# Squared-ReLU attention and top-1 experts on one core: end-of-chunk steps, start and order of the mixed steps rearranged

## The chip, the core and the metric

The kernel runs on one core of a Trainium2 chip. The metric is device time in microseconds (us); lower is better. The core has the engines TensorE (PE in the rows, with PEld for its weight loads), VectorE (DVE), ScalarE (ACT), GpSimd (POOL) and SyncE (SP, which issues most DMAs). Each takes its instructions in the order of its own queue.

## What is computed

With B = 8, S = 2496, D = 256, 64 query columns, E = 8 experts, capacity 80 and F = 1024:

```
scores = (1/S) * z @ z.T          # z [B, S, 64]
attn   = max(scores, 0) ** 2
x      = u * (attn @ v)           # u, v [B, S, 256]
idx    = argmax(x @ w_gate), gate = its softmax weight
per expert: the 80 tokens of the largest gate,
    out[tok] = gate * (max(x[tok] @ w1[e], 0) @ w2[e])
```

## The kernel before

**Tiling.** A *chunk* is 512 query columns of one batch (`b`, `qc` from 0 to 4; the fifth, `qc` = 4, has 448), 40 chunks in all. Its keys are 20 tiles of 128 rows, taken as 10 *pairs*. For a pair PE makes the scores (`scores`, matmuls L399, or L461 where only a half is needed), ACT the relu (L402) and the square (L405), ACT or DVE the rounded high part `ah` (L408, or L413 and L475 on DVE), and DVE the remainder `al` = a - ah (helper line L55). v is split likewise into two parts in `vt` (ACT L108, DVE L159). The scores are symmetric, so a block that another chunk needs too is transposed on DVE (L304, L316), written to DRAM, read back later (`blk`, `shared`) and only cast there (ACT L376, L471).

**Attention.** `attend_half` (L544) multiplies a pair in two *groups* of 12 matmuls: group 0 takes the passes with `ah` and then those with `al`, group 1 the `al` passes first. A matmul reads half the rows of a tile, so that two run side by side on the upper and lower half of the array; group 1 swaps which PSUM bank each half adds to, and waits for group 0 through an empty POOL instruction (L550). The two `acc` banks of a chunk are summed and multiplied by u at its end: `chunk_x_first` (DVE L569) reads one bank, `chunk_x_copy` (ACT L584) the other. The next chunk but one takes these banks over.

**Order of the work.** PE, ACT, DVE and SP follow an order that is written out by hand. After five opening steps with one chunk alone (`HALF` = 5) two *lanes* run side by side, the even chunks in the first and the odd ones in the second, shifted by half a chunk. A step `t` takes one pair of each lane (entries `e` and `e + 1`) and prepares two others (`e + 3`, `e + 4`): `begin` issues scores and relu, `middle` the square and the ACT cast of `ah`, `low` the DVE part (`al`), `turn` the transposes. Chunks end every fifth step; where an even one ends, `low(e + 3)` stands ahead of `chunk_x_first`, and where an odd one ends, the cast in `middle(e + 4)` stands ahead of `chunk_x_copy`. `z_and_v` splits z (`prep_zs`: L121 and L55 twice, 64 partitions each) and then v. `finish` spreads the rest of a chunk's end (`xb`, the second part of x, and the gate's logits, L684, reduced in L698) over the next chunk's steps. In 56 steps (14 of the half chunks, 4 steps each) one lane is 448 wide and the other 512; they are called mixed here.

**Start and end.** At the start 9 matmuls on zeros (`warm`, L186) precede the first scores, and `first` handles two pairs like any other. The last chunks run alone (`attend`, L515). The expert stage follows: GpSimd fetches each expert's rows by an indirect DMA (`token`, L1589) that DVE copies (L110, in `whole`), while the gate's last part (L744 to L771) and weight loads (L861) run.

Of the kernel before, what the change touches and what calls it, by code (L numbers as in the profile page):

```python
# [8 lines left out]
F32 = mybir.dt.float32  # L9
# [17 lines left out]
def attn_moe_kernel(ctx, tc, zT, uT, v, wg, w1, w2, out, seq, cap):  # L27
# [73 lines left out]
    def load_z(b, j):  # L101
        raw = zpool.tile([P, CH], F32, tag="zraw", name=f"zraw_{nid()}", bufs=1)
        nc.sync.dma_start(out=raw, in_=zT[b, :, j * CH:(j + 1) * CH])
        return raw

# [75 lines left out]
    nc.gpsimd.memset(idle, 0.0)  # L181

    def warm(n, pool, tag):
        wm = pool.tile([P, CH], F32, tag=tag, name=f"warm_{nid()}")
        for i in range(n):
            nc.tensor.matmul(wm, idle[:, :P], idle, start=True, stop=True)  # L186

    warm(9, ps_m, "m")
    raw12 = upool.tile([P, 2, CH], F32, tag="ut", name="raw12")
    nc.sync.dma_start(out=raw12[:, 0], in_=zT[0, :, CH:2 * CH])  # L190
    vraw0 = load_v(0, 0)
    nc.sync.dma_start(out=raw12[:, 1], in_=zT[0, :, 2 * CH:3 * CH])
    vraw1 = load_v(0, 1)
    raw34 = xpool.tile([P, 2, CH], F32, tag="xf", name="raw34")
    nc.sync.dma_start(out=raw34, in_=zT[0, :, 3 * CH:].rearrange("p (j t) -> p j t", j=2))
# [6 lines left out]
    wg_r = const.tile([P, DC, E], F32, name="wg_r")  # L202
# [22 lines left out]
    def constants_v():  # L225
        V.tensor_copy(out=wgs[:, :, 0], in_=wg_sb)
# [158 lines left out]
    def scores(b, qc, k):  # L385
# [18 lines left out]
        def square():  # L404
            nc.scalar.activation(out=a[:, :, :nc_], in_=a[:, :, :nc_], func=AF.Square)  # L405
            st["ah"] = pair_tile("ah", b, qc, k, bufs=4)
            if not on_v:
                nc.scalar.copy(out=st["ah"][:, :, :nq], in_=a[:, :, :nq])  # L408
# [18 lines left out]
        return square, low, turn  # L427
# [5 lines left out]
    def scores_rest(b, qc, k):  # L433
# [32 lines left out]
        def square():  # L466
            nc.scalar.activation(out=a, in_=a, func=AF.Square)
            st["ah"] = pair_tile("ah", b, qc, k, bufs=4)
# [17 lines left out]
        return square, low, None  # L486
# [32 lines left out]
    def attend_half(b, qc, p, group):  # L519
# [13 lines left out]
        for i, (k, x, a) in enumerate(mm):  # L533
            if start_up and i == len(ks):
                warm(2, ps_m, "m")
# [100 lines left out]
    def chunk_rows_last(b, qc):  # L636
# [16 lines left out]
        for ts_ in (slice(0, 2), slice(2, n)):  # L653
            nc.sync.dma_start(out=rows[r0 + ts_.start * P:r0 + ts_.stop * P].rearrange("(t p) w -> p t w", p=P),
                              in_=xq[:, ts_].rearrange("p t h d -> p t (h d)"))
        nc.sync.dma_start(out=rows[r0 + n * P + P - TAIL:r0 + QT * P],
                          in_=xq[P - TAIL:, n].rearrange("p h d -> p (h d)"))
# [31 lines left out]
    def chunk_sum(b, qc):  # L689
# [3 lines left out]
        for h, pl in enumerate(parts):  # L693
            o = lg_t[b][:, qc * QT:(qc + 1) * QT]
            if h:
                o = gp.tile([P, NT, E // 2], F32, tag="s4", name=f"lg2_{b}_{qc}")
                o = o.rearrange("p t e -> p (t e)")[:, :QT * E].rearrange("p (t e) -> p t e", e=E)
# [151 lines left out]
    def load_raw(e, which, part, after=None):  # L849
# [7 lines left out]
        if after:  # L857

            after.memset(raw[:, :1], 0.0)
        rv, src = raw_part(raw, e, which, part)  # L860
        nc.sync.dma_start(out=rv, in_=src)  # L861
# [16 lines left out]
    def loads(n, after=None):  # L878
        n = min(n, NR - len(ready) - len(halves))
        for p in pieces[:n]:  # L880
            ready.append((p, load_raw(*p, after)))
        del pieces[:n]
# [183 lines left out]
    if True:  # L1066
        prep_zm(0, 0, raw0)
# [25 lines left out]
        def middle(i):  # L1093
            b, qc, r = entries[i]
            if computed(i):
                pending[i][0]()
            else:
                pending[i] = None, mirrored(b, qc, 2 * pairs_of[b, qc][r]), None

        def low(i):  # L1100
            pending[i][1]()

        def turn(i):
            if pending[i][2]:
                pending[i][2]()
            del pending[i]

        def whole(i):
            begin(i)
            middle(i)  # L1110
            low(i)
# [13 lines left out]
        def z_and_v(t):  # L1125
# [3 lines left out]
            zb = b if tm < 2 else b + 1  # L1129
            if 0 < zb < B:  # L1130
# [5 lines left out]
            vb = b if tm < NP else b + 1  # L1136
            if 0 < vb < B:
                if tm in V_SPLIT:
                    g = V_SPLIT[tm]
                    prep_v(vb, g, v_raw.pop((vb, g)), nc.scalar, V)  # L1140
                if tm in V_LOAD:
                    v_raw[vb, V_LOAD[tm]] = load_v(vb, V_LOAD[tm])
# [22 lines left out]
        def group(i, g):  # L1165
            b, qc, r = entries[i]
            attend_half(b, qc, pairs_of[b, qc][r], g)
# [5 lines left out]
        for t in range(HALF):  # L1173
            if t == 0:
                begin(2)
            group(t, 0)
# [3 lines left out]
            first_parts(t)  # L1180
            group(t, 1)
# [6 lines left out]

        for t in range(HALF, END):
            e = HALF + 2 * (t - HALF)  # L1190
            n_end = t // HALF - 1 if t % HALF == HALF - 1 else None
            begin(e + 3)
            middle(e + 3)
            group(e, 0)
# [19 lines left out]
            low(e + 4)  # L1214
# [6 lines left out]
        for i in range(e, len(entries)):  # L1221
# [8 lines left out]
            if i == e + HALF + 1:  # L1230
                logits(n)
            if i + 2 < len(entries) and i > e:
# [5 lines left out]
            if i < e + HALF:  # L1238
                for j in range(2):
                    finished(*at(n), 2 * (i - e) + j)  # L1240
                    if i > e or j:
                        finished(*at(n - 1), NP + 2 * (i - e) + j)
# [200 lines left out]
    def steps_of(own, tl, tw, ps_t, ps_h):  # L1443
# [37 lines left out]
        def places_():  # L1481


            for n in ("cnt", "exc", "rin", "base"):
                small[n] = tl.tile([P, E], F32, name=f"{n}_all")
            for e in range(E):
# [31 lines left out]
        def many_rows():  # L1518
            le = le_g[1][:, :, 1:]
            tt(le, le, tot[:, es], ALU.mult)  # L1520
            V.tensor_reduce(out=small["exc"][:, es], in_=le, axis=AX.X, op=ALU.add)
# [55 lines left out]

        def token(i):
# [9 lines left out]
            xg = tw.tile([P, 2, D], U16, tag="xg", name=f"xg_{i}{own}", bufs=6)  # L1588
            nc.gpsimd.indirect_dma_start(  # L1589
# [3 lines left out]
            xg_t[i] = [xg, tok, j]  # L1593

        def target(i):
# [4 lines left out]
            xg, tok, j = xg_t[i]  # L1600
# [120 lines left out]
        def flags_end():  # L1721
            flags2(ps_t, "t")

        early_steps = (ps_t, ps_h, (ffn1_high, ffn1_low), places_, one_block, one_within, (many_blocks, many_counts, many_rows, many_within,
                       many_pe, many_fetch), pe_block, pe_fetch, warm_up, flags_v, flags_end, x_t, sl)
# [27 lines left out]
    def ahead(early_steps, steps):  # L1753
# [3 lines left out]
         flags_v, flags_end, x_t, sl) = early_steps  # L1757
        many_blocks, many_counts, many_rows, many_within, many_pe, many_fetch = many
# [21 lines left out]
        PL = nc.gpsimd  # L1780
        FIRST_J, LAST_J = range(FC // 2), range(FC // 2, FC)
        with tc.manual_schedule(engines={ET.Pool}):
# [17 lines left out]
            many_pe()  # L1800
            gate_near(B - 1, NQ - 1)
            gate_sum(B - 1, NQ - 1, NQ)
            whole(0)
            gate_store(P, NCOL - P, ps_t, "t")
            ffn_x(0)
            many_counts()
            many_fetch((2,))
            ffn_xl(0)
            ffn1(0, 0)
            whole(1)  # L1810
            many_rows()
            many_within()
            token(2)
            ffn_x(1)
            ffn_xl(1)
            ffn1(0, 1)
            token(3)
            loads(4, PL)
            ffn_h(0, 0)
            many_fetch((4, 6))  # L1820
            ffn1(1, 0)
            empty()
            target(0)
            target(1)
            token(4)
# [4 lines left out]
            ffn_x(2)  # L1830
            ffn_xl(2)
# [6 lines left out]
            spread(3)  # L1838
            for i in range(2, NU):
# [9 lines left out]
                if i == 2:  # L1849
                    token(6)  # L1850
                    token(7)
# [6 lines left out]
                if i + 1 < NU:  # L1858
                    cast(2)
                    lows(2)  # L1860
                ffn2(i - 1, FIRST_J)
# [58 lines left out]
```

## Time and profile before

| what | value |
|---|---|
| median of 3 runs | 1353.8 us (1351.98 to 1354.32) |
| profiled execution | 1355.23 us |
| its span, first to last instruction | 1353.3 us |
| mean granted TensorE clock | 0.993 of full |
| PE busy | 1329.6 us (98%) |
| DVE busy | 1085.8 us (80%) |
| ACT busy | 1020.1 us (75%) |

The profile is read by stage: the share of PE over the whole span says only that PE has work nearly all the time. The views used below are the page's busy times, the list of waits (which engine line stood idle for which other, in total, times, longest), windows (busy time of each engine in one stretch) and the timeline, whose rows give the start, the duration, and in brackets the idle time before with what ended it.

### The profile page before, as it was taken

The numbers are of one execution on the slowest core, as the hardware profiler recorded it, in microseconds if no ns is written. First come the engines' busy times: TensorE is split into PE (matmuls) and PEld (weight loads), VectorE is DVE, ScalarE is ACT, GpSimd is POOL, SyncE is SP. The second block draws the span as 40 slices with busy tenths as digits, with TensorE's granted clock in tenths as the row PEclk, the third lists the DMA queues.
The fourth block names the chain that finished last, engine by engine and source line by source line (L and its number), as shares of the span: only waits on it lengthen the run. The fifth ranks groups of instructions, "written<-read, shape, count | busy, mean of one in ns | idle before, by whom it ended". The sixth has DMA issues, their size and how long they took to land.

```text
span 1353.3 us, 32346 instructions
## 1 busy us (share of the span) xinstructions
PE 1329.6 (98%) x12887; PEld 1210.7 (89%) x12887; DVE 1085.8 (80%) x1667; ACT 1020.1 (75%) x1361; POOL 40.1 (3%) x42
## 2 busy tenths in 40 slices
PE   8999999999999999999999999999999999999997
PEld 5789998999899997999889998999889998898776
DVE  6777888887887888878878888878888778777886
ACT  6776787677867787776877778776877678777666
POOL 0000000000000000000000000000000000000065
PEclk8999999999999999999999999999999999999999
DMA  5799989999899998999899998999979997989945
GB/s 164 223 269 258 283 224 289 241 277 244 259 239 250 290 262 227 270 247 261 222 262 269 257 285 225 260 264 261 249 237 243 286 267 214 290 226 274 272 136 188
DMA packets 286013, 337.12 MB, mean 249 GB/s; under 512 B 96824, under 2 KB 206368, under 8 KB 275616
## 3 DMA queue, kind: packets, MB, share of 16 engines
q1 hardware_dynamic: 284832, 333.68, 93.8%
q8 instruction: 103, 1.69, 0.5%
q0 software_dynamic: 1024, 1.31, 0.3%
q14 instruction: 54, 0.44, 0.1%
HBM read 162.67 MB, written 135.48 MB: 220 GB/s over the span
## 4 chain that ended last, share of the span: by engine, by line
PE 83%; DVE 6%; ACT 4%; DMA 4%; issue 2%; SPq 0%; POOL 0%; DVEq 0%; POOLq 0%; ACTq 0%
PE acc L544 69%; PE s L399 9%; PE pl L684 2%; ACT a L402 1%; ACT a L405 1%; DVE al L55 1%; DMA blk<-y 1%; PE s L461 1%; DMA wraw<-w 1%; DVE x L304 1%; DVE vt L159 1%; PE warm L186 0%; ACT xf L584 0%; DMA y<-x 0%; PE op L1699 0%
## 5 line engine op out<-in xcount | busy, mean ns | idle before, releaser
L544 PE MATMUL acc<-ah,vt 64*128 64x512 f32 (+1 forms) x6004 | 845.9, 387 | 6.3 <-DVE xf L569 3.7
L544 PEld LDWEIGHTS acc<-ah,vt 64*128 64x128 f32 x6004 | 660.0, 185 | 60.1 <-DVE xf L569 6.7
L544 PE MATMUL acc<-al,vt 64*128 64x512 f32 (+1 forms) x3002 | 503.9, 389 | 0.4 <-DVE al L55 0.2
L55 DVE TENSOR_TENSOR al<-a,ah 128x1024 fp32r<-128x1024 f32 (+2 forms) x240 | 272.3, 1135 | 174.4 <-ACT ah L408 76.7
L544 PEld LDWEIGHTS acc<-al,vt 64*128 64x128 f32 x3002 | 340.0, 185 | 23.5 <-DVE al L55 1.1
L402 ACT ACTIVATE a<-s 128x512 f32<-128x512 f32 (+1 forms) x408 | 221.0, 594 | 141.7 <-PE s L399 138.8
L376 ACT CAST ah<-blk 128x1024 fp32r<-128x1024 f32 x160 | 167.1, 1047 | 102.7 <-PE acc L544 94.2
L55 DVE TENSOR_TENSOR al<-blk,ah 128x1024 fp32r<-128x1024 f32 x160 | 193.4, 1214 | 38.2 <-PE acc L544 10.7
L405 ACT ACTIVATE a<-a 128x1024 f32<-128x1024 f32 x204 | 216.3, 1060 | 6.3
L304 DVE STREAM_TRANSPOSE x<-a 128x512 f32<-128x512 f32 x320 | 207.6, 687 | 0.0
L408 ACT CAST ah<-a 128x1024 fp32r<-128x1024 f32 x160 | 168.0, 1050 | 5.8 <-PE acc L544 0.8
L399 PE MATMUL s<-zm,zs 64*128 64x512 f32 x960 | 148.7, 392 | 4.1 <-ACT a L402 4.1
L399 PEld LDWEIGHTS s<-zm,zs 64*128 64x128 f32 x960 | 107.2, 185 | 14.3 <-ACT a L402 5.7
L1589 POOL DMA_INDIRECT xg<-xs,tok x8 | 13.0, 1630 | 1294.7 <-ACT w2h L888 1286.1
L159 DVE TENSOR_TENSOR vt<-vraw,vt 128x1024 fp32r<-128x1024 f32 (+1 forms) x40 | 46.3, 1156 | 1.6 <-ACT vt L108 1.3
L55 DVE TENSOR_TENSOR xf<-xf,xb 128x1024 f32<-128x1024 f32 (+1 forms) x38 | 45.2, 1189 | 0.4
L55 DVE TENSOR_TENSOR xb<-xf,xb 128x1024 bf16<-128x1024 f32 (+1 forms) x38 | 45.1, 1186 | 0.2
L108 ACT CAST vt<-vraw 128x1024 fp32r<-128x1024 f32 (+3 forms) x56 | 44.9, 830 | 0.0
L594 ACT CAST xb<-xf 128x1024 bf16<-128x1024 f32 (+1 forms) x39 | 39.8, 1020 | 5.0 <-DVE xf L55 2.8
L602 ACT CAST xb<-xf 128x1024 bf16<-128x1024 f32 (+1 forms) x38 | 38.8, 1020 | 5.4 <-DVE xf L55 5.4
L399 PE MATMUL s<-zm 64*128 64x512 f32 x264 | 42.3, 400 | 0.4 <-ACT a L402 0.4
L413 DVE CAST ah<-a 128x1024 fp32r<-128x1024 f32 (+1 forms) x44 | 29.7, 675 | 14.1 <-ACT a L405 14.1
(190 smaller groups left out, 905.9 us busy)
## 6 DMA issues: line engine op xcount, KB each, us to landing
y<-x SPq DMA_DIRECT2D x80, 1024.0 KB, 6.9
blk<-y SPq DMA_DIRECT2D x320, 256.0 KB, 6.9
out<-idle SPq DMA_DIRECT2D x40, 512.0 KB, 7.8
vraw<-v SPq DMA_DIRECT2D x32, 512.0 KB, 9.3
zm<-zs SPq DMA_DIRECT2D x128, 128.0 KB, 4.8
ut<-uT SPq DMA_DIRECT2D x32, 512.0 KB, 6.8
xs<-xq SPq DMA_DIRECT2D x32, 512.0 KB, 6.6
wraw<-w SPq DMA_DIRECT2D x28, 512.0 KB, 5.3
```

What stands on the lines that cost most here:

```text
L55: V.tensor_tensor(out=o, in0=a, in1=b, op=op)
L108: eng.copy(out=o, in_=i)
L159: e1.tensor_tensor(out=vt[:, :nf, 1], in0=raw[:, :nf], in1=vt[:, :nf, 0], op=ALU.subtract)
L304: V.transpose(out=x[:, :, :, t].rearrange("p n k s -> p k n s"), in_=a)
L376: nc.scalar.copy(out=natural(ah), in_=src)
L399: nc.tensor.matmul(s, zk, zm[rows, :, y].rearrange("p h k t -> p k h t"), start=i == 0, stop=i == 2)
L402: nc.scalar.activation(out=a[:, h, :nc_], in_=s[:, :nc_], func=AF.Relu)
L405: nc.scalar.activation(out=a[:, :, :nc_], in_=a[:, :, :nc_], func=AF.Square)
L408: nc.scalar.copy(out=st["ah"][:, :, :nq], in_=a[:, :, :nq])
L544: ins = nc.tensor.matmul(acc[c], vt, mv, start=p == pairs[0] and group == 0 and i == 0, stop=p == pairs[-1] and group == 1 and i == len(mm ...
L594: nc.scalar.copy(out=xb[:, 0], in_=xf)
L602: nc.scalar.copy(out=xb[:, 1], in_=xr)
```

## The change

- The first pair's work is written anew (`first_pair`): relu, square and cast are divided between ACT and DVE, v is split in two halves, the warm-up has 8 matmuls and needs a smaller memset, scores stand inside the first group where two warm-up matmuls stood.
- z is loaded in two DMAs of 64 partitions that fetch only the halves which are used, and `prep_zs` splits 128 partitions at once: 2 DVE instructions where there were 4.
- `middle` is cut in two, the square and the cast. At the end of an odd chunk the cast follows `chunk_x_copy`; at the end of an even chunk `low(e + 3)` follows `chunk_x_first`; `z_and_v` splits v ahead of z.
- In a mixed step the second lane's second group, with its `low`, `turn`, `first_parts` and `z_and_v`, moves into the next step, behind `begin(e + 3)`, and the next step's first group is issued ahead of that.
- In the closing part `chunk_store`, `chunk_hi` and `chunk_lo` of the chunk that ended are taken earlier. In the expert stage the first rows are fetched ahead of the gate's last part, a small indirect DMA runs on GpSimd before, the four weight loads wait for the fourth fetch (`xg_t[3]`) and `token(6)`, `token(7)` come later.

```diff
     def prep_zs(b, j, raw):
-        for h in range(2):
-            rows = slice(h * HP, (h + 1) * HP)
-            src = tiles_of(raw)[rows, :, h]
-            V.tensor_copy(out=zs[rows, 0], in_=src)
-            tt(zs[rows, 1], src, zs[rows, 0], ALU.subtract)
+        src = raw.rearrange("p (k t) -> p k t", t=P)
+        V.tensor_copy(out=zs[:, 0], in_=src)
+        tt(zs[:, 1], src, zs[:, 0], ALU.subtract)
...
+    def first_pair(v_high, v_low):
...
+        nc.scalar.activation(out=a[:, 0], in_=ss[0], func=AF.Relu)
+        ts(a[:, 1], ss[1], 0.0, ALU.max)
+        v_high(0)
+        nc.scalar.activation(out=a[:, 0], in_=a[:, 0], func=AF.Square)
+        tt(a[:, 1], a[:, 1], a[:, 1], ALU.mult)
+        nc.scalar.copy(out=ah[:, 0], in_=a[:, 0])
+        V.tensor_copy(out=ah[:, 1], in_=a[:, 1])
+        v_low(0)
+        al = pair_tile("al", 0, 0, 0)
+        tt(al, a, ah, ALU.subtract)
...
-        first = scores(0, 0, 0)
-        first[0]()
-        first[1]()
-        prep_v(0, 0, vraw0, nc.scalar, V)
-        first = scores(0, 0, 2)
-        first[0]()
-        first[1]()
+        first_pair(v_high, v_low)
+        second_pair = scores(0, 0, 2)
+        v_high(1)
+        second_pair[0]()
+        v_low(1)
+        second_pair[1]()
+        second_pair[2]()
...
+        def second_lane(t):
+            e = HALF + 2 * (t - HALF)
+            group(e + 1, 1)
+            low(e + 4)
+            turn(e + 4)
+            first_parts(t)
+            z_and_v(t)
+
+        def mixed(t):
+            return t // HALF % NQ in (0, NQ - 1) and t % HALF < HALF - 1
+
         for t in range(HALF, END):
...
+            if t == HALF:
+                group(e, 0)
             begin(e + 3)
+            if mixed(t - 1):
+                second_lane(t - 1)
             middle(e + 3)
-            group(e, 0)
+            cast(e + 3)
+            if t > HALF and not mixed(t - 1):
+                group(e, 0)
...
             group(e, 1)
-            low(e + 3)
             if n_end is not None and n_end % 2 == 0:
                 chunk_x_first(*at(n_end))
                 chunk_x_copy(*at(n_end))
+            low(e + 3)
             turn(e + 3)
             middle(e + 4)
+            second = n_end is not None and n_end % 2 == 1
+            if not second:
+                cast(e + 4)
             finish(t, 1)
             transfers(e + 1)
+            if mixed(t):
+                group(e + 2, 0)
+                continue
             group(e + 1, 1)
-            if n_end is not None and n_end % 2 == 1:
+            if second:
                 chunk_x_first(*at(n_end))
                 chunk_x_copy(*at(n_end))
+                cast(e + 4)
             low(e + 4)
...
-            gate_near(B - 1, NQ - 1)
-            gate_sum(B - 1, NQ - 1, NQ)
             whole(0)
...
-            loads(4, PL)
             ffn_h(0, 0)
+            gate_store(P, NCOL - P, ps_t, "t")
+            loads(4, xg_t[3][3])
```

On DVE where chunk (0, 4), an even one, ends (names end in batch, chunk, pair; the trailing number is a counter). Before:

```order
184 L55 TENSOR_TENSOR xb_0_3_2274<-xf_0_3_2273,xb_0_3_2274 128x1024
185 L475 CAST ah_1_0_2_2699<-a_1_0_2_2687 128x512
186 L55 TENSOR_TENSOR al_1_0_2_2759<-a_1_0_2_2687,ah_1_0_2_2699 128x512
187 L55 TENSOR_TENSOR al_1_0_2_2759<-shared_137,ah_1_0_2_2699 128x512
188 L569 SCALAR_TENSOR_TENSOR xf_0_4_2762<-acc_0_4_0_1846,ut_0_4_2457 128x448
189 L413 CAST ah_1_1_4_2767<-a_1_1_4_2735 128x1024
```

and with the change:

```order
171 L55 TENSOR_TENSOR xb_0_3_2267<-xf_0_3_2266,xb_0_3_2267 128x1024
172 L610 SCALAR_TENSOR_TENSOR xf_0_4_2751<-acc_0_4_0_1840,ut_0_4_2452 128x448
173 L516 CAST ah_1_0_2_2705<-a_1_0_2_2673 128x512
174 L55 TENSOR_TENSOR al_1_0_2_2756<-a_1_0_2_2673,ah_1_0_2_2705 128x512
175 L55 TENSOR_TENSOR al_1_0_2_2756<-shared_140,ah_1_0_2_2705 128x512
176 L429 CAST ah_1_1_4_2760<-a_1_1_4_2728 128x1024
```

The read of the bank (L569, now L610) stood behind three instructions of `low` and now stands ahead of them.

On ACT where chunk (1, 0), an odd one, ends. Before:

```order
224 L405 ACTIVATE a_1_1_12_3246<-a_1_1_12_3246 128x1024
225 L408 CAST ah_1_1_12_3272<-a_1_1_12_3246 128x1024
226 L584 ACTIVATE xf_1_0_3280<-acc_1_0_1_2309 128x512
227 L376 CAST ah_1_2_2_3291<-blk_1_2_0_2974 128x1024
228 L402 ACTIVATE a_1_1_14_3323<-s_1_1_14_3324 128x512
```

and with the change:

```order
225 L419 ACTIVATE a_1_1_12_3238<-a_1_1_12_3238 128x1024
226 L625 ACTIVATE xf_1_0_3270<-acc_1_0_1_2304 128x512
227 L424 CAST ah_1_1_12_3274<-a_1_1_12_3238 128x1024
228 L390 CAST ah_1_2_2_3284<-blk_1_2_0_2968 128x1024
229 L416 ACTIVATE a_1_1_14_3316<-s_1_1_14_3317 128x512
```

The copy of the other bank (L584, now L625) and the cast have changed places.

On PE in a mixed step, where the second group of the 448 wide chunk's pair 0 ends. Before:

```order
1232 L544 MATMUL acc_0_4_1_1847<-ah_0_4_0_1728,vt_0_0_170 128x448
1233 L544 MATMUL acc_0_4_0_1846<-ah_0_4_0_1728,vt_0_0_170 128x448
1234 L544 MATMUL acc_0_3_0_1386<-al_0_3_16_1807,vt_0_4_673 128x512
1235 L544 MATMUL acc_0_3_1_1387<-al_0_3_16_1807,vt_0_4_673 128x512
1236 L544 MATMUL acc_0_3_0_1386<-al_0_3_16_1807,vt_0_4_673 128x512
```

and with the change:

```order
1226 L585 MATMUL acc_0_4_1_1841<-ah_0_4_0_1722,vt_0_0_149 128x448
1227 L585 MATMUL acc_0_4_0_1840<-ah_0_4_0_1722,vt_0_0_149 128x448
1228 L585 MATMUL acc_0_4_1_1841<-ah_0_4_2_1810,vt_0_0_149 128x448
1229 L585 MATMUL acc_0_4_0_1840<-ah_0_4_2_1810,vt_0_0_149 128x448
1230 L585 MATMUL acc_0_4_1_1841<-ah_0_4_2_1810,vt_0_0_149 128x448
```

The other lane's second group (`acc_0_3`) followed here; now the same lane's next pair comes first, and `acc_0_3` follows behind that and the next scores.

## Rows read from the trace of the kernel before

**Rows 1.** The list of waits (us in total, times, longest us).

```profile
PEld acc L544 <- DVE xf L569: 6.7, 10, 1.9
PEld acc L544 <- ACT xf L584: 5.5, 10, 0.6
PEld acc L544 <- DVE vt L159: 3.0, 4, 0.9
```

**Rows 2.** Timeline of the end of chunk (0, 4), an even one.

```profile
193.06 0.42 DVE L475 CAST ah<-a 128x512 fp32r<-128x512 f32 x1
...
193.88 1.07 PE L399 MATMUL s<-zm,zs 64*128 64x512 f32 x6
...
194.79 0.62 DVE L569 SCALAR_TENSOR_TENSOR xf<-acc,ut 128x448 f32<-128x448 f32 x1
...
195.47 0.77 PEld L544 LDWEIGHTS acc<-ah,vt 64*128 64x128 f32 x8 [0.96 <-DVE xf L569]
```

**Rows 3.** Timeline of the end of chunk (1, 0), an odd one.

```profile
227.62 1.05 ACT L408 CAST ah<-a 128x1024 fp32r<-128x1024 f32 x1
...
228.71 1.69 PE L544 MATMUL acc<-ah,vt 64*128 64x512 f32 x8
...
230.02 0.85 PE L544 MATMUL acc<-al,vt 64*128 64x512 f32 x4
```

**Rows 4.** Timeline of a split of v behind one of z.

```profile
337.19 0.24 DVE L121 CAST zs<-zraw 64x256 fp32r<-64x256 f32 x1
...
338.68 1.22 DVE L159 TENSOR_TENSOR vt<-vraw,vt 128x1024 fp32r<-128x1024 f32 x1
...
339.96 0.53 PEld L544 LDWEIGHTS acc<-ah,vt 64*128 64x128 f32 x6 [0.70 <-DVE vt L159]
```

**Rows 5.** Timeline of the start.

```profile
1.39 4.02 PE L186 MATMUL warm<-idle 128*128 128x512 bf16 x9 [1.39 <-POOL idle L181]
...
4.17 0.69 DVE L55 TENSOR_TENSOR zm<-zraw,zm 128x512 fp32r<-128x512 f32 x1
...
5.34 1.91 PE L399 MATMUL s<-zm 64*128 64x512 f32 x7
...
20.46 1.08 ACT L402 ACTIVATE a<-s 128x512 f32<-128x512 f32 x2 [4.17 <-PE s L399]
```

**Rows 6.** Groups by line and shape (count, then busy us and mean ns).

```profile
L405 ACT ACTIVATE a<-a 128x1024 f32<-128x1024 f32 x202 | 214.4, 1062 | 6.2
...
L569 DVE SCALAR_TENSOR_TENSOR xf<-acc,ut 128x512 f32<-128x512 f32 x33 | 22.6, 687 | 3.0 <-PE acc L544 2.8
...
L467 ACT ACTIVATE a<-a 128x512 f32<-128x512 f32 x29 | 18.4, 633 | 0.9
...
L475 DVE CAST ah<-a 128x512 fp32r<-128x512 f32 x29 | 12.1, 416 | 0.0
```

**Rows 7.** Windows: busy us of PE, PEld, DVE, ACT, POOL, clock, DMA share, GB/s.

```profile
6.90:10.30 3.40, 1.33 (x9) 0.63 (x6) 1.03 (x2) 3.24 (x5) 0.00 (x0) 1.00 0.89 317
10.30:17.20 6.90, 6.39 (x23) 3.61 (x25) 6.07 (x9) 5.90 (x8) 0.00 (x0) 0.51 0.46 131
...
144.00:158.00 14.00, 14.00 (x132) 14.00 (x130) 12.31 (x17) 8.89 (x11) 0.00 (x0) 1.00 1.00 279
```

**Rows 8.** Timeline of PE: an unmixed stretch, then a mixed one.

```profile
107.24 1.15 PE L544 MATMUL acc<-ah,vt 64*128 64x512 f32 x8
...
110.95 1.17 PE L544 MATMUL acc<-ah,vt 64*128 64x512 f32 x8
...
147.53 1.18 PE L544 MATMUL acc<-ah,vt 64*128 64x512 f32 x8
...
152.78 1.16 PE L544 MATMUL acc<-ah,vt 64*128 64x512 f32 x8
```

**Rows 9.** Timeline of the closing part and of the expert stage.

```profile
1253.59 0.62 PEld L684 LDWEIGHTS <-xb 128*128 128x128 bf16 x22 [1.19 <-DVE xb L55]
...
1301.38 0.45 DVE L110 COPY xf<-xg 80x512 uint16<-80x512 uint16 x1 [1.73 <-DMA xg<-xs,tok]
```

More of the change, by code (lines that the diff above doesn't have):

```diff
@@ L180, in attn_moe_kernel @@
     idle = const.tile([P, CH], BF16, name="idle")
-    nc.gpsimd.memset(idle, 0.0)
+    nc.gpsimd.memset(idle[:, :P], 0.0)
     def warm(n, pool, tag):
@@ L185, in warm @@
         for i in range(n):
[L186 to L192, printed above, removed]
+            nc.tensor.matmul(wm, idle[:, :P], idle[:, :P].rearrange("p (o t) -> p o t", o=1).broadcast_to([P, QT, P]),
+                             start=True, stop=True)
+    warm(8, ps_m, "m")
+    nc.gpsimd.memset(idle[:, P:], 0.0)
+    raw12 = upool.tile([P, 2, CH // 2], F32, tag="ut", name="raw12")
+    load_sides(raw12[:, 0], 0, 1, 2)
+    vraw0 = keep.tile([P, QT, D], F32, tag="vraw", name="vraw_0_0")
+    for h in range(2):
+        nc.sync.dma_start(out=vraw0[:, 2 * h:2 * h + 2],
+                          in_=v[0, 2 * h * P:(2 * h + 2) * P, :].rearrange("(t p) d -> p t d", p=P))
+    load_sides(raw12[:, 1], 0, 2, 3)
     vraw1 = load_v(0, 1)
-    raw34 = xpool.tile([P, 2, CH], F32, tag="xf", name="raw34")
-    nc.sync.dma_start(out=raw34, in_=zT[0, :, 3 * CH:].rearrange("p (j t) -> p j t", j=2))
+    raw34 = xpool.tile([P, 2, CH // 2], F32, tag="xf", name="raw34")
+    load_sides(raw34.rearrange("p j t -> p (j t)"), 0, 3, 5)
     ident = const.tile([P, P], F32, name="ident")
@@ L426, in scores @@
         on_v = k // QT == qc
-        return square, low, turn
+        return square, cast, low, turn
+    def first_pair(v_high, v_low):
+        zm = zm_t[0, 0]
+        a = pair_tile("a", 0, 0, 0, F32, 2)
+        ah = pair_tile("ah", 0, 0, 0, bufs=4)
+        ss = [ps_s.tile([P, CH], F32, tag="s", name=f"s_0_0_{h}") for h in range(2)]
+        for i, (x, y) in enumerate(((0, 0), (1, 0), (0, 1))):
+            for h, s in enumerate(ss):
+                rows = slice(h * HP, (h + 1) * HP)
+                nc.tensor.matmul(s, zm[rows, h, x, 0], zm[rows, :, y].rearrange("p h k t -> p k h t"),
+                                 start=i == 0, stop=i == 2)
+        nc.scalar.activation(out=a[:, 0], in_=ss[0], func=AF.Relu)
[8 more added lines that the diff above has]
+        tt(al, a, ah, ALU.subtract)
+        a_t[0, 0, 0] = (ah, al)
     def two_parts(x):
@@ L484, in low @@
                 folded.add((b, qc, k))
-        return square, low, None
+        return square, cast, low, None
     acc_t = {}
@@ L533, in attend_half @@
         for i, (k, x, a) in enumerate(mm):
-            if start_up and i == len(ks):
-                warm(2, ps_m, "m")
+            if start_up and i == 2 * len(ks):
+                between()
             for h in range(2):
@@ L652, in chunk_rows_last @@
         n = QT - 1
[L653 to L657, printed above, removed]
+        late["stored"] = [nc.sync.dma_start(
+            out=rows[r0 + ts_.start * P:r0 + ts_.stop * P].rearrange("(t p) w -> p t w", p=P),
+            in_=xq[:, ts_].rearrange("p t h d -> p t (h d)")) for ts_ in (slice(0, 2), slice(2, n))]
+        late["stored"].append(nc.sync.dma_start(out=rows[r0 + n * P + P - TAIL:r0 + QT * P],
+                                                in_=xq[P - TAIL:, n].rearrange("p h d -> p (h d)")))
     def chunk_store2(b, qc):
@@ L847, in raw_part, with load_raw @@
         return raw.rearrange("p (c f) -> p c f", c=n // 2), src[:, part * n // 2:(part + 1) * n // 2]
-    def load_raw(e, which, part, after=None):
+    def load_raw(e, which, part, behind=None):
         pool, tag = keep, "vraw"
@@ L856, in load_raw @@
         raw = pool.tile([P, NPIECE // 2], F32, tag=tag, name=f"wraw_{e}_{which}_{part}")
-        if after:
-            after.memset(raw[:, :1], 0.0)
         rv, src = raw_part(raw, e, which, part)
-        nc.sync.dma_start(out=rv, in_=src)
+        ins = nc.sync.dma_start(out=rv, in_=src)
+        if behind:
+            after(ins, behind)
         return rv
@@ L876, in attn_moe_kernel, with loads @@
     pieces, ready = [], []
-    def loads(n, after=None):
+    def loads(n, behind=None):
         n = min(n, NR - len(ready) - len(halves))
         for p in pieces[:n]:
-            ready.append((p, load_raw(*p, after)))
+            ready.append((p, load_raw(*p, behind)))
         del pieces[:n]
@@ L1110, in whole @@
             middle(i)
+            cast(i)
             low(i)
@@ L1129, in z_and_v @@
             zb = b if tm < 2 else b + 1
+            vb = b if tm < NP else b + 1
+            if 0 < vb < B and tm in V_SPLIT:
+                g = V_SPLIT[tm]
+                prep_v(vb, g, v_raw.pop((vb, g)), nc.scalar, V)
             if 0 < zb < B:
@@ L1180, in attn_moe_kernel @@
             first_parts(t)
+            cast(t + 2)
             group(t, 1)
@@ L1485, in places_ @@
                 small[n] = tl.tile([P, E], F32, name=f"{n}_all")
+            xg_t[0] = rows_tile(0)
+            late["stored"].append(nc.gpsimd.memset(xg_t[0][:num(0)], 0))
+            ready = nc.gpsimd.engine_nop()
+            for x in late["stored"]:
+                after(ready, x)
             for e in range(E):
@@ L1576, in within, with rows_tile @@
             sl[i] += [rin, base]
+        def rows_tile(i):
+            return tw.tile([P, 2, D], U16, tag="xg", name=f"xg_{i}{own}", bufs=6)
         def token(i):
@@ L1830, in ahead @@
             ffn_x(2)
+            spread(3)
             ffn_xl(2)
```

132 lines of the change are left out of this document (79 added, 53 removed).

## Prediction

> **What bounds the kernel now.** The page's busy times come first: TensorE has matmuls in flight in nearly all of the span, so only two things can shorten it, fewer matmul cycles or fewer moments in which the next matmul waits. The change removes no attention matmul, so I went to the list of waits and read who keeps TensorE's weight loader idle [rows 1]: three releasers, each an instruction of another engine that stands late in its own queue. The timeline then shows each case once [rows 2 to 4]. The reader is to see that the releaser is not slow but queued: work that nobody needs yet stands ahead of it. Last come the two ends, where TensorE really idles: the start [rows 5, 7] and the stage of the closing chunks and experts [rows 9].
>
> The sum is made against one profiled execution of 1355.2 us, which lies 1.4 above the median of the runs shown, 1353.8. All terms are differences, so I take them off the median. A change of less than 0.2%, 2.7 us, counts as no change: the three runs themselves lie 2.3 apart.
>
> **Ends of even chunks.** The scores of the next step start at 193.88 and are 6 matmuls. At 0.116 us each (3.71 us for the 32 matmuls from 107.24 to 110.95 [rows 8]) the next group should start at 194.58; it starts at 195.47 [rows 2], 0.89 late, because VectorE reads the bank from 194.79 only. Three instructions of another pair stand in front of that read, from 193.06 on. With the change the read takes the place at 193.1 and ends at 193.7, before TensorE asks. The same pattern stands at 508, 822 and 1137 us, so 4 x 0.89 = 3.6. A longer one, at 70 us, is the longest of its kind, 1.9 by the loader [rows 1]; the matmul is late by somewhat less, 1.7. Together **5.3**. What is late next is `low`: its `al` ends 0.6 later, and its first reader is TensorE a whole step (over 5 us) later. I cost that at nothing; uncovered it would be 0.6 at 5 places, 3.
>
> **Ends of odd chunks.** ScalarE's copy waits behind a 1.05 us cast. From 228.71 to 230.02 TensorE starts 8 matmuls in 1.31 where 8 x 0.116 = 0.93 would do: 0.38 late [rows 3]. The list has ten such waits, 0.55 each by the loader [rows 1]; scaled like this one, 10 x 0.38 to 0.41, **4.0**. The copy then ends 1.05 earlier than before, more than the delay, so all of it goes. The cast and the subtraction behind it come 0.6 later, which the lane's next group (2.8 us off) hides.
>
> **v ahead of z.** The subtraction that finishes v starts at 338.68 behind four z instructions that began at 337.19; the loader waits 0.70 for it [rows 4]. Less the 0.07 to 0.17 by which a loader's wait exceeds the matmul's (0.96 against 0.89, 0.55 against 0.38), some 0.55. Three of the four waits of this kind lie in the steps, the fourth in the start: **1.6**. z is needed only for scores of the next batch and can wait 1.2. The two z instructions that remain are as long in columns as two of the old four, so DVE also saves 0.7 per split, which lies beside TensorE's work.
>
> **The start.** I follow ScalarE, the longest chain. The warm-up's 9 matmuls took 4.02, 0.447 each, the length of the lower clock level (1.2 GHz). Eight take 3.6 and start near 1.0 with the smaller memset: over by 4.6. The first scores then wait for zm, ready at 4.86, and take 6/7 of 1.91: until 6.5 [rows 5]. ScalarE: half a relu (half of 1.08) and half a v cast, square and `ah` cast at 0.63 each [rows 6]: 8.9. Relu, half a v cast and square of the second pair (1.08, 0.63, 1.06): 11.7. Relu, square, a v cast and an `ah` cast of the third (1.08, 1.06, 1.05, 1.05): 15.9. There the relu of the fourth pair can start, which before started at 20.46, after an idle 4.17 in which it waited for scores [rows 5]. TensorE at the upper level has those scores by 14.8: 8 matmuls until 9.85, scores by 10.7, 16 matmuls by 12.6, then the next pair's first group, whose `al` VectorE has by 13.6 (11.7 + 0.69 + 1.23), and 6 scores. So **4.6**.
>
> Two prices here are new. A relu on VectorE out of PSUM has no row. The nearest, on 128x512, are a cast in 0.42 and the bank's read in 0.69 [rows 6]; I take 0.69, since it reads PSUM too. ScalarE's chain hides either end, so neither changes the sum; were the read 0.69 longer still, it would be up to 0.3 less. The z loads are cut into two DMAs of half as many bytes together; I cost them at nothing, with 0.5 either way.
>
> The clock matters more. The rows show it granted in full from 6.9 to 10.3, with TensorE busy 1.33 of 3.40, and at 0.51 from 10.3 to 17.2 [rows 7]. The new order leaves TensorE fewer holes there (scores, 8 matmuls, scores: some 2.3 of 3.4), so I take the upper level, without certainty.
>
> The Trainium skill, page "TensorE: Matmul & The Clock Gate", section "What's actually happening", says that the default state is throttled and activity releases it; by that the start keeps the lower level if its holes are still too large. The fall at 10.3 behind a stretch with TensorE busy 1.33 of 3.40 agrees with it [rows 7]. By that rule the term would be 2.1 in place of 4.6 (first rival).
>
> **Closing part and experts.** The logits' loader waits 1.19 for a VectorE subtraction at 1253.6 [rows 9]; taken earlier it costs nothing: **1.2**. In the expert stage the third fetch lands late, and VectorE idles 1.73 for it [rows 9] while four weight loads are in flight. These loads now wait for the fetches, so up to 1.73 may come back; but the same loads then land later, and casts of weights wait for them. Bounds -2 and +2; I take **0.5**, the gate's instructions that now stand behind the first copy.
>
> **The mixed steps.** An unmixed matmul takes 0.116, so 24 of 512 columns and 24 of 448 should take 24 x 0.116 x 1.875 = 5.22. The mixed stretch takes 5.25 from 147.53 to 152.78 [rows 8]. Half of the changes of width go; at most 0.015 per step and 56 steps: 0 to 0.8. I take 0. No wait appears there either: TensorE and its loader are busy 14.00 of 14.00 [rows 7].
>
> **Sum.** 5.3 + 4.0 + 1.6 + 4.6 + 1.2 + 0.5 + 0 = 17.2; 1353.8 - 17.2 = 1336.6, forecast **1337**.
>
> **Rivals.**
> 1. *The start keeps the lower clock.* From 10.3 to 17.2 every matmul takes twice as long. Scores until 11.4, 4 and 12 matmuls until 15.2, the next group until 17.6, scores until 18.3: the fourth relu is 2.1 earlier, not 4.6. Against it speak the smaller holes, for it that the old start fell there too. 1339 to 1340.
> 2. *The waits only move.* What was put behind is late next: `al` at even ends, `ah` at odd ends, z behind v. Then only start, closing part and experts gain: 4.6 + 1.2 + 0.5 = 6.3, 1347.5. For it: VectorE is busy in most of these stretches. Against it: each moved piece has a whole step before it is read.
> 3. *The mixed order brings its own wait (slower).* A lane's second group is now followed by its next pair's first, whose `ah` and `al` must be ready one group earlier; and the second lane's `low` stands behind the next scores. VectorE is busy 12.31 of 14.00 in a mixed stretch [rows 7], the fullest in the kernel, so slack is smallest there. At 0.31 per step (17.2 / 56) the whole gain is gone; with waits like those at odd ends, 0.38, it is 56 x 0.38 = 21, 1358. Against it: the loader stands still nowhere in that stretch, and an `al` is wanted two or three groups of 1.4 (12 x 0.116) sooner, not a whole step.
> 4. *It does not do what it says.* The order of the instructions shows each of the moves; only the start could be late for another reason, a load of v in two halves that lands after 7: 1341.
>
> **How the numbers follow.** The forecast's case has 0.60, rival 1 0.15, rival 2 0.12, rival 3 0.10, rival 4 0.03. The low end, 1331: experts +1.5 over the forecast, the mixed order 0.8, a start better by 1, shorter idle in the steps up to 60 us by 0.7, the spread of the runs 2. The high end, 1347: rival 1 (2.5) with the experts' lower bound (2.5), and a good half of what rival 2 takes (5.5 of 10.9). Rival 3 and the rest of rival 2 are left out. Slower 0.08: 0.07 of rival 3 and 0.01 of rival 4, for a load that is late throughout. The same 0.05: 0.03 of rival 3, with a wait of 0.26 to 0.36 per step, and 0.02 of rival 2, with the start failing too. Faster 0.87: all the rest.
>
> **What would show it.** Right: no wait of the loader for the reading of the banks above 0.2, the fourth relu near 16, the clock without a second low stretch before 20, TensorE's first group near 9, a mixed pair of steps again at 5.2. The prediction is wrong if the list of waits names `al` or `ah` for more than 3 us in the steps, if the mixed steps take over 5.4 per two, or if the expert stage, from its first fetch to the end, is longer than before.

## The result and the profile after

| | before | after |
|---|---|---|
| median of 6 runs | 1353.9 us (1352.0 to 1354.3) | **1311.2 us** (1309.8 to 1312.5) |
| profiled execution | 1355.2 | 1312.4 |
| its span | 1353.3 | 1310.5 |
| PE busy | 1329.6 (98%) | 1295.4 (99%) |

The ratio is 0.9688, 95% interval 0.9675 to 0.9700. The change takes 42.7 us away. Forecast were 17, range 7 to 23: right in sign, wrong in size by 2.5 times.

The page of after, its busy times, its clock row and its costliest group:

```profile
PE 1295.4 (99%) x12884; PEld 1203.6 (92%) x12884; DVE 1062.0 (81%) x1606; ACT 1016.4 (78%) x1362; POOL 38.8 (3%) x45
...
PEclk9999999999999999999999999999999999999999
...
L585 PE MATMUL acc<-ah,vt 64*128 64x512 f32 (+1 forms) x6004 | 793.0, 382 | 1.0 <-ACT ah L461 0.6
```

The last row held the first surprise. Before, the same 6004 matmuls stood there with 845.9 us:

```profile
L544 PE MATMUL acc<-ah,vt 64*128 64x512 f32 (+1 forms) x6004 | 845.9, 387 | 6.3 <-DVE xf L569 3.7
```

No attention matmul had been taken out, and all waits together [rows 1] could not pay for it. (The busy time of this group overlaps with that of its `al` half, so the 52.9 between the two rows are not themselves the gain.) The list of waits of after, where [rows 1] had three releasers of the loader:

```profile
PEld acc L585 <- DVE al L55: 1.4, 3, 0.6
...
PEld acc L585 <- ACT ah L461: 1.0, 1, 1.0
...
PEld acc L585 <- DVE ah L429: 0.8, 1, 0.8
```

The waits for the banks' readers (now L610 and L625) and for v are gone, as forecast. They cannot be all of it: TensorE also got faster where it had waited for nothing. The timeline of PE in an unmixed stretch of after, to be held against [rows 8]:

```profile
109.24 0.66 PE L585 MATMUL acc<-al,vt 64*128 64x512 f32 x4
109.69 1.12 PE L585 MATMUL acc<-ah,vt 64*128 64x512 f32 x8
110.60 0.66 PE L585 MATMUL acc<-al,vt 64*128 64x512 f32 x4
```

From the first row's start to the last row's start are 12 matmuls, 1.36 us; before, the same groups took 1.39 to 1.40. Per two matmuls that run side by side this is 227 ns against 233. How many of these matmuls are 512 wide:

```profile
L585 PE MATMUL acc<-ah,vt 64*128 64x512 f32 x4912 | 666.6, 386 | 1.0 <-ACT ah L461 0.6 <-DVE ah L429 0.4
L585 PE MATMUL acc<-al,vt 64*128 64x512 f32 x2456 | 403.0, 389 | 0.3
```

That is 7368, or 614 groups of 12, and 614 x 0.035 = 21.5, most of what the forecast lacked. Why a matmul that waits for nothing becomes 2.5% faster is the question of the experiments.

The start, for [rows 5]:

```profile
4.61 1.65 PE L454 MATMUL s<-zm 64*128 64x512 f32 x6
...
6.32 0.69 DVE L59 TENSOR_SCALAR a<-s 128x512 f32<-128x512 f32 x1 [0.81 <-PE s L454]
...
8.62 1.19 PE L585 MATMUL acc<-ah,vt 64*128 64x512 f32 x8 [0.59 <-ACT ah L461]
...
14.89 1.07 ACT L416 ACTIVATE a<-s 128x512 f32<-128x512 f32 x2
```

And windows of after (columns as in [rows 7]): the two of the start, the mixed stretch, the first stretch and the next of the closing part's logits, and the expert stage:

```profile
6.90:10.30 3.40, 2.64 (x19) 1.91 (x21) 3.17 (x6) 3.37 (x7) 0.00 (x0) 1.00 0.94 225
10.30:17.20 6.90, 6.77 (x60) 5.23 (x59) 6.17 (x9) 6.80 (x10) 0.00 (x0) 1.00 0.63 168
...
144.00:158.00 14.00, 14.00 (x178) 14.00 (x176) 11.00 (x14) 9.65 (x14) 0.00 (x0) 1.00 1.07 298
...
1218.60:1222.00 3.40, 1.61 (x30) 1.40 (x29) 3.32 (x4) 1.79 (x2) 0.00 (x0) 1.00 1.21 189
1222.00:1225.40 3.40, 3.40 (x12) 2.55 (x10) 3.00 (x5) 1.40 (x3) 0.00 (x0) 0.51 1.05 290
...
1245.55:1310.50 64.95, 56.48 (x397) 45.49 (x396) 49.69 (x108) 43.68 (x78) 34.68 (x24) 0.95 0.50 168
```

The granted clock stays up through the start (1.00 where it was 0.51) and falls in a new place, at 1222.

### The profile page after: what moved, and what is told of

It is laid out like the page before. It is cut to its first block, busy times and chain, and to the rows that moved or that the text cites. A ratio compares the mean times of both kernels' runs of the same rounds, so it can differ in the third digit from the quotient of the medians.

```text
span 1310.5 us, 32301 instructions
## 1 busy us (share of the span) xinstructions
PE 1295.4 (99%) x12884; PEld 1203.6 (92%) x12884; DVE 1062.0 (81%) x1606; ACT 1016.4 (78%) x1362; POOL 38.8 (3%) x45
## 4 chain that ended last, share of the span: by engine, by line
PE 90%; DVE 3%; ACT 2%; DMA 2%; issue 2%; SPq 0%; POOL 0%; POOLq 0%; ACTq 0%; DVEq 0%
PE acc L585 75%; PE s L413 10%; PE pl L725 2%; DMA blk<-y 1%; PE acc L556 1%; PE s L500 1%; DVE w1l L935 1%; ACT a L416 1%; DMA xs<-xq 1%; DVE w2l L935 0%; DMA xq<-xf 0%; ACT a L419 0%; PE warm L195 0%; ACT ah L424 0%; ACT w1h L927 0%
## 5 line engine op out<-in xcount | busy, mean ns | idle before, releaser
L585 PE MATMUL acc<-ah,vt 64*128 64x512 f32 (+1 forms) x6004 | 793.0, 382 | 1.0 <-ACT ah L461 0.6
L585 PEld LDWEIGHTS acc<-ah,vt 64*128 64x128 f32 x6004 | 644.4, 184 | 35.5 <-ACT ah L461 1.0
L585 PE MATMUL acc<-al,vt 64*128 64x512 f32 (+1 forms) x3002 | 476.6, 384 | 0.3
L585 PEld LDWEIGHTS acc<-al,vt 64*128 64x128 f32 x3002 | 323.0, 184 | 18.4 <-DVE al L55 1.4
L416 ACT ACTIVATE a<-s 128x512 f32<-128x512 f32 x406 | 220.4, 596 | 107.6 <-PE s L413 100.6
L413 PE MATMUL s<-zm,zs 64*128 64x512 f32 x960 | 143.2, 387 | 0.9 <-ACT a L416 0.9
L413 PEld LDWEIGHTS s<-zm,zs 64*128 64x128 f32 x960 | 104.2, 184 | 8.3 <-ACT a L416 2.2
L625 ACT ACTIVATE xf<-acc 128x512 f32<-128x512 f32 (+1 forms) x38 | 22.3, 586 | 29.6 <-PE acc L585 26.0
L610 DVE SCALAR_TENSOR_TENSOR xf<-acc,ut 128x512 f32<-128x512 f32 (+3 forms) x44 | 28.1, 646 | 19.6 <-PE acc L585 19.1
L413 PE MATMUL s<-zm 64*128 64x512 f32 x258 | 39.1, 392 | 0.4 <-DVE a L59 0.4
```

Source lines behind the costliest of these rows:

```text
L413: nc.tensor.matmul(s, zk, zm[rows, :, y].rearrange("p h k t -> p k h t"), start=i == 0, stop=i == 2)
L416: nc.scalar.activation(out=a[:, h, :nc_], in_=s[:, :nc_], func=AF.Relu)
L585: ins = nc.tensor.matmul(acc[c], vt, mv, start=p == pairs[0] and group == 0 and i == 0, stop=p == pairs[-1] and group == 1 and i == len(mm ...
```

## The experiments

The diff holds two more edits, which the cut diff ahead of the prediction leaves out, and so did the prediction's sum. A gate constant (`wg_r`) moves into a buffer that exists anyway, and the last batches' logits get a buffer of their own instead of borrowing the tag `s4`:

```diff
-    wg_r = const.tile([P, DC, E], F32, name="wg_r")
...
+        wg_r = gp.tile([P, NT, E], F32, tag="d", name="wg_r")[:, :DC]
...
-                o = gp.tile([P, NT, E // 2], F32, tag="s4", name=f"lg2_{b}_{qc}")
-                o = o.rearrange("p t e -> p (t e)")[:, :QT * E].rearrange("p (t e) -> p t e", e=E)
+                o = gp.tile([P, QT, E], F32, tag="lg2", name=f"lg2_{b}_{qc}")
```

Neither adds or removes work. But they shift the addresses of all tiles that are allocated behind them. The addresses below are those that the program's allocator gives, in bytes within a partition, modulo 512; the trace does not show them. Of an attention matmul the *weights* are a tile of `vt` and the *streamed* tile is `ah` or `al`. The *distance* is that between their starts, modulo 256, as the shorter way round; 0, 32, 64, 128 and 256 were tried, no others.

The theories, as they came up:
- **Order** (2 in the expectations): the pace comes from the new order of the instructions.
- **Alignment** (1): from the starts' own alignment, that of the streamed tiles (1a) or of the weights (1b).
- **Distance** (3): from the distance alone.

The table is in the order of the text below; every ratio is against before on the same chip, with its 95% interval, and the pace is that of 12 matmuls in an unmixed stretch.

| run | weights, streamed | distance | pace, us | time, us | ratio |
|---|---|---|---|---|---|
| before | 448, 320 | 128 | 1.39 | 1353.9 | 1 |
| after, again | 384, 384 | 0 | 1.36 | 1310.3 | 0.968 [0.966, 0.970] |
| before, `wg_r` moved | 384, 256 | 128 | 1.39 | 1354.0 | 1.000 [0.999, 1.001] |
| after, both moves undone | 448, 320 | 128 | 1.40 | 1333.7 | 0.985 [0.983, 0.987] |
| after, streamed tiles off | 384, 320 | 64 | 1.40 | 1334.1 | 0.986 [0.984, 0.988] |
| after, weights off | 448, 384 | 64 | 1.40 | 1335.3 | 0.986 [0.984, 0.988] |
| before, both moves | 384, 384 | 0 | 1.36 | 1338.6 | 0.989 [0.986, 0.992] |
| after, logits' move undone | 384, 256 | 128 | 1.40 | 1332.9 | 0.985 [0.983, 0.987] |
| after, both off alike | 320, 320 | 0 | 1.36 | 1314.7 | 0.972 [0.970, 0.974] |
| after, 256 apart | 224, 480 | 0 (256) | 1.36 | 1319.1 | 0.974 [0.972, 0.976] |
| after, 32 apart | 384, 416 | 32 | 1.40 | 1333.9 | 0.986 [0.984, 0.988] |
| after, only `ah`, `al`, x shifted | 384, 416 | 32 | 1.40 | 1336.6 | 0.987 [0.985, 0.989] |
| after, no mixed order | 384, 384 | 0 | 1.36 | 1313.2 | 0.971 [0.969, 0.972] |

**Before with `wg_r` moved.** One move alone, in the old order: the first two lines of the diff above, without the others.

> The kernel before with one part of the change alone: the 64 byte tile wg_r no longer stands in the pool const but in a buffer of gp that exists already. No instruction moves. All tiles behind it, so v, ah, al, zm and zs, then begin at a multiple of 128 bytes in a partition; before they began 64 bytes beside one. Theory 1 (the place of the tiles sets the matmul's pace): the two matmuls that run side by side come every 227 ns, not every 233, and the time falls by some 26 us, to about 1328. Theory 2 (the new order of the instructions brings the pace, wg_r is nothing): 1354, 233 ns.

Nothing changed: 1354.0, and the pace is the old one, 12 matmuls in 110.74 - 109.35 = 1.39:

```profile
109.35 0.72 PE L544 MATMUL acc<-al,vt 64*128 64x512 f32 x4
...
110.74 0.72 PE L544 MATMUL acc<-al,vt 64*128 64x512 f32 x4
```

The starts are multiples of 128 here as in after, so that is not what decides. Order and distance both survive.

**After with both moves undone, with the streamed tiles off, with the weights off.** All three have the new order. The first puts `wg_r` and the logits back. The second keeps `wg_r` moved and the third puts it back; both put the logits back and add 64 bytes:

```diff
+    pad = gp.tile([P, 16], F32, tag="pad", name="pad")
```

> The changed kernel with the tiles moved back beside the multiple of 128 bytes: wg_r stands in const again and lg2 shares the buffer of s4 as before; v, ah, al, zm and zs are all 64 bytes off. Theory 1: the matmul pairs come every 233 ns again, some 26 us more than the changed kernel's 1311, so about 1337, which is what the other parts of the change give alone. Theory 2: 1311 and 227 ns.

> The changed kernel with v (the weights of the attention) at a multiple of 128 bytes, but ah, al and zm (what is streamed through), and zs and a, 64 bytes off. Theory 1a (the streamed operand's place counts): 233 ns per pair and about 1337. Theory 1b (the weights' place counts): 227 ns in attention, where the weights are v, and 233 in the scores, whose weights are zm and zs; scores are a ninth of the matmuls, so about 1314. Theory 2: 1311.

> The changed kernel with v and the blocks read back 64 bytes off, but ah, al, zm and zs at a multiple of 128 bytes: the mirror image of the run before. Theory 1a (streamed operand): 227 ns and 1311. Theory 1b (weights): 233 ns in attention and about 1334. Theory 2: 1311.

1333.7, 1334.1 and 1335.3, with the old pace in each. So the pace is not the new order's (theory 2 falls), and either tile can spoil it, whichever of them keeps its start of after (1a and 1b fall). What remains is that the two starts stand in some relation.

**Before with both moves, and after with one undone.** The first has the old order and exactly the starts of after. The second takes only the logits' move back.

> The kernel before with two parts of the change that move no instruction but tiles: wg_r in gp and lg2 in a buffer of its own. Each tile that TensorE reads then stands at the very address of the changed kernel (v and ah both 384 behind a multiple of 512; with wg_r alone they were at 384 and 256). Theory 3 (the distance of the weights' tile from the streamed tile, modulo 256 or 512, sets the pace): 227 ns and about 1353.7 - 26 = 1328. Theory 2 (the order of the instructions and the layout are needed together, or the order alone): 233 ns and 1354.

> The changed kernel with lg2 in s4's buffer as before: v at 384, ah, al, zm, zs at 256 behind a multiple of 512, all at a multiple of 128, distance 128. Theory 3: about 233 ns and 1334, as the other three altered ones had. Theory 1 (a multiple of 128 is enough): 227 ns and 1311.

The old order gets the fast pace, 1.36:

```profile
109.39 0.64 PE L544 MATMUL acc<-al,vt 64*128 64x512 f32 x4
...
110.75 0.64 PE L544 MATMUL acc<-al,vt 64*128 64x512 f32 x4
```

and the new order without the logits' buffer loses it, 1.40:

```profile
110.59 0.72 PE L585 MATMUL acc<-al,vt 64*128 64x512 f32 x4
...
111.99 0.73 PE L585 MATMUL acc<-al,vt 64*128 64x512 f32 x4
```

This splits the gain. Order alone: 1332.9 against 1352.3 on that chip, 19.4. Addresses alone: 1338.6, so 13.7, where 1328 was expected. Addresses on top of the order: 1332.9 to 1310.3, 22.6. The two help each other, and the list of waits of the old order at the new pace says how:

```profile
PEld acc L544 <- DVE xf L569: 11.0, 18, 2.1
...
PEld acc L544 <- ACT xf L584: 6.4, 10, 0.6
...
PEld acc L544 <- DVE vt L159: 4.1, 5, 1.0
```

These are the same three releasers as in [rows 1], with 21.5 instead of 15.2: VectorE and ScalarE are no faster, and a TensorE that comes sooner waits longer. Of the 8.9 that the old order gives back (22.6 - 13.7), these waits show 6.3.

**Both off alike, and 256 apart.** The first shifts weights and streamed tiles by the same 64 bytes, which puts neither where after has it; the second sets them 256 apart (further constants packed into one tile, 256 bytes added). The edit of the first:

```diff
-    slot = const.tile([P, NST], F32, name="slot")
...
-    sl_x = const.tile([P, NST], F32, name="sl_x")
-    sl_lo = const.tile([P, NST], F32, name="sl_lo")
+    slots = const.tile([P, 3, NST], F32, name="slots")
+    slot, sl_x, sl_lo = (slots[:, x] for x in range(3))
```

> The changed kernel with all tiles moved down by 64 bytes together (three small constants share one tile): v, ah, al, zm and zs at 320 behind a multiple of 512, distance 0, none at a multiple of 128. Theory 3 (only the distance counts): 227 ns and 1311. Theory 1 or a mixture (each must be at a multiple of 128): 233 ns and 1334.

> The changed kernel with v at 224 and ah, al, zm, zs at 480 behind a multiple of 512 bytes, distance 256 (small constants share a tile, 256 bytes are put between). Theory 3 with a period of 256: 227 ns and 1311 as at distance 0. With a period of 512: another pace, 233 ns and 1334 if every distance other than 0 costs the same, and in any case not 227.

Both have the fast pace. The rows are of the second, 109.72 - 108.36 = 1.36:

```profile
108.36 0.71 PE L584 MATMUL acc<-al,vt 64*128 64x512 f32 x4
...
109.72 0.71 PE L584 MATMUL acc<-al,vt 64*128 64x512 f32 x4
```

So among the starts that were tried the attention's pace goes by the distance, and a distance of 256 counts as none. The times, 1314.7 and 1319.1, lie 4 and 9 above after, so 1311 was missed both times. By the profiled executions the first run (1313.5) is only 1.1 behind after (1312.4) and had lost 1.6 by 48 us: its first 12 attention matmuls took 3.36, those of after 2.48. For the second some of it is waits in the steps, among them two of the loader for ACT's copies of x, 2.5 together. What sets either off was not found.

**32 apart, two ways.** The first shifts the streamed tiles with all that lies behind the pad (like the run 256 apart, it also keeps the experts' gate values in one tile). The second puts the pad into the pool of `ah`, `al` and the x tiles, so that weights, z and the tiles of the blocks stay.

```diff
+    pad = upool.tile([P, 8], F32, tag="pad", name="pad")
```

> The changed kernel with v at 384 and ah, al, zm, zs at 416 behind a multiple of 512, distance 32. If any distance within 64 bytes counts as the same place: 227 ns and 1311. If the distance must be 0: 233 ns and about 1334, as at distances 64 and 128.

> The changed kernel with only ah, al (and the tiles of x behind them) moved by 32 bytes: v, zm, zs, a and blk stay at 384 behind a multiple of 512, ah and al stand at 416. Theory 3, read as the two operands of one matmul: attention's distance is 32, so 233 ns there and about 20 us more than 1311, near 1331. If instead the place of z, of a or of the blocks made the difference in the earlier runs: 227 ns and 1311.

The old pace in both, 1333.9 and 1336.6. (The second was expected near 1331; in its profiled execution the clock is at half from 1263.5 to 1277.2, longer than in any other run.) The rows of the second, 111.84 - 110.44 = 1.40:

```profile
110.44 0.69 PE L586 MATMUL acc<-al,vt 64*128 64x512 f32 x4
...
111.84 0.70 PE L586 MATMUL acc<-al,vt 64*128 64x512 f32 x4
```

A shift of one of the two by 32 bytes is enough. Distances 32, 64 and 128 all give 233 ns per two matmuls, 0 and 256 give 227; there is no step between. Both runs keep the logits' own buffer, so it is not that buffer as such which brings the pace.

One rival the addresses leave: the blocks that are read back (`blk`) start where `vt` does, modulo 512, in every run, so a cast from `blk` to `ah` on ScalarE is at the same distance. The opening steps settle it. Of after:

```profile
14.67 0.62 PE L585 MATMUL acc<-al,vt 64*128 64x512 f32 x4
...
16.94 0.62 PE L585 MATMUL acc<-al,vt 64*128 64x512 f32 x4
```

and of the run with the logits' move undone:

```profile
14.69 0.66 PE L585 MATMUL acc<-al,vt 64*128 64x512 f32 x4
...
17.02 0.64 PE L585 MATMUL acc<-al,vt 64*128 64x512 f32 x4
...
42.83 1.05 ACT L390 CAST ah<-blk 128x1024 fp32r<-128x1024 f32 x1 [3.83 <-DMA blk<-y]
```

These are 20 matmuls in 2.27 and in 2.33, the two paces, long before the first block is cast at 42.83.

But the distance inside a matmul is not the whole cause. The scores read only `zm` and `zs`, which start at the same remainder in every run, so their own distance is always 0. Still their pace goes along: by the starts in the traces two scores side by side take on average 227.5 to 227.8 ns in the six runs at the fast pace, and 230.4 to 232.2 in seven of the eight at the slow one (227.8 in the eighth, the first of these two runs). What a matmul's neighbours read therefore seems to count too; how was not tested.

**After without the mixed order**, all else and all addresses as in after; and after itself again.

```diff
         def mixed(t):
-            return t // HALF % NQ in (0, NQ - 1) and t % HALF < HALF - 1
+            return False
```

> The changed kernel without the new order in the 56 mixed steps (mixed() is always false); layout and all else as in the change. The prediction's reading (the order of widths is worth 0 to 0.8 us): 1311 to 1312. If the new order is worth more at the faster pace, for instance because it saves waits there: 1313 or above. If it costs (its third rival): below 1310.

> The changed kernel, not altered, beside the three others. v, ah, al and zm all begin 384 bytes behind a multiple of 512. All theories: 1311 and 227 ns per pair of matmuls; were it 1334 and 233 ns, the pace would be a matter of the chip or of the hour and not of the program.

1313.2 (1312.7 to 1314.0) against 1310.3 (1309.7 to 1312.5), each beside before on its own chip: the mixed order seems worth 2 to 3 us. The ratios' intervals overlap a little (0.966 to 0.970 and 0.969 to 0.972), so by the times alone the size is loose. The traces agree: where VectorE reads a bank for the last time before the closing part (1201.8 in before), the run without the mixed order is 41.7 ahead of before and after is 44.0, and most of these 2.3 build up evenly through the steps. Where it comes from was not found.

## Why the prediction was wrong

**The step that failed** stands in its part on the mixed steps: "An unmixed matmul takes 0.116", read off the trace of before and carried over to after as it was. The terms above it were waits and the work at the two ends. The two moved tiles had no term at all: they shift the addresses of what TensorE reads, and the sum took its pace as fixed. Measured, the pace went from 1.40 to 1.36 per 12 matmuls, worth 22.6 us, over half of the gain. The reason is shown as far as the addresses: moving tiles without moving an instruction changes the pace, and for attention the distance of the weights' tile from the streamed one tells which of the two paces it is. What happens inside TensorE or the memory, and why the scores go along, is not shown.

**The rest, by the run with the new order and the old pace** (the logits' move undone). It gained 19.4 where 17.2 was summed. Its PE timeline against the other two, at the first single-lane matmul of the closing part; of before:

```profile
1235.02 0.73 PE L515 MATMUL acc<-ah,vt 128*128 128x512 f32 x2
```

of that run:

```profile
1214.20 0.74 PE L556 MATMUL acc<-ah,vt 128*128 128x512 f32 x2
```

and of after:

```profile
1191.09 0.73 PE L556 MATMUL acc<-ah,vt 128*128 128x512 f32 x2
```

So 20.8 up to there by order, and 23.1 more by pace (between profiled executions; that of before lies 1.4 above its median). Point by point:

- *Ends of even and odd chunks, v ahead of z* (5.3 + 4.0 + 1.6): right. All these waits are gone. By the starts of the chunks this run gains 3.3 per two batches; the terms make 2.6 of it (0.89 for one even end, 3 x 0.4 for the odd ends, 0.55 for one v). The rest, 0.35 per batch or some 2 in all, agrees with what the mixed order is worth.
- *The start* (4.6): right in kind, 1.0 short. The fourth relu starts at 14.89 where 15.9 was worked out, 5.6 earlier than before. The relu on VectorE took 0.69, as taken. The clock kept its upper level (1.00 from 10.3 to 17.2), so rival 1 fell; none of the eleven profiled executions with the new start fell there. That the smaller holes are the reason was not isolated, and the old start does not fall each time: before with `wg_r` moved had 1.00 there too, and its fourth relu started at 17.13. Against that execution the new start gains 2.2, not 5.6; the term holds against an execution that falls.
- *Up to 60 us* (0.7, only in the range): some 2.0.
- *Closing part* (1.2): the wait of [rows 9] is gone, but another of its kind appears at the next logits, 0.5 to 1.6 in the six runs with the new order and the old pace. In after it is

```profile
1220.68 0.71 PE L725 MATMUL pl<-wgs,xb 128*128 128x24 bf16 x22 [1.79 <-DVE xb L55]
```

  From the first single-lane matmul to the first fetch before took 53.6. This run took 52.1, the six 52.0 to 54.4, with 0.9 saved by their median. After took 54.5, and behind that wait its clock falls to 0.51 from 1222.0 to 1225.4 (windows above), so some of what the pace had won is lost here again. The pace alone does not decide the fall. It is there in after, in its repetition, in 256 apart and, at the old pace, in the run with the weights off; both off alike and the run without the mixed order have the fast pace and no fall.
- *Expert stage* (0.5): nothing of it is seen. From the first fetch to the end it takes 64.95 (the last window above) against 64.64 before. The sign by which the prediction called itself wrong is met by 0.3, but 12 of the 14 profiled executions, old order and new, lie between 64.3 and 65.4, so 0.3 says nothing either way.
- *Mixed steps* (0): too low by some 2, though a mixed pair of steps looks as forecast: from 137.92 to 143.09 in the timeline of after, 48 matmuls in 5.17 [rows 8].
- *Rival 2* (waits move) fell: `al` and `ah` keep the loader waiting 3.2 in all, 1.0 of it in the start and the rest before 46 us. *Rival 3* (the mixed order waits) fell: it gains. *Rival 4* fell.

Had pace been a term, the sum would have been 17.2 + 21.5 = 38.7, 1315, 0.3% from the result. That this comes so close is in part luck: the steps up to 60 us, the start and the mixed order gave some 5 more than the sum had, and the closing part and the expert stage, where 1.7 was to be gained, together lost 1.1.

## What to carry to other kernels

When a diff moves, drops or resizes even a small tile, compare the addresses of what TensorE reads before any wait is costed, and try weights and streamed tiles at the same remainder modulo 256; here that was worth 2.5% of each attention matmul 512 wide. Hold a steady group of matmuls of both traces side by side first: if its pace differs, waits do not explain the gain. Removed waits and a faster pace add up to more than each alone, since the engine that got faster finds the other queues as late as they were (here 13.7 by pace in the old order, 22.6 in the new).

## What was not expected of the hardware

- The pace of attention matmuls that wait for nothing depends on where their tiles lie to each other: 227 ns per two at distances 0 and 256, 233 at 32, 64 and 128, in either order of the instructions. The scores slow down with them, though their own tiles lie at distance 0. The groups 448 wide hardly show it: by the starts in the traces 203 ns per two before, 202 after.
- A kernel can meet a fall of the clock that it did not have before: 0.51 for 3.4 us in after, behind a stretch with TensorE busy 1.61 of 3.40. Four of the eleven profiled executions of the changed kernel and its variants have it in the closing part, at either pace.
- The old start has the fall in some executions only: from 10.3 to 17.2 the clock was 0.51 in before, 0.75 in before with both moves, 1.00 in before with `wg_r` moved.
